# A retention layer and two gated products: the head of the kernel reordered, state scaling moved to ScalarE, a gate clipped from PSUM

## The chip, the cores and the metric

The kernel runs on one core of a Trainium2 chip. The metric is device time of one execution in microseconds. The engines are TensorE (PE, with its weight loads as PEld), VectorE (DVE), ScalarE (ACT), GpSimd (POOL) and SyncE (SP), whose queue issues nearly all transfers.

## The reference

A retention layer over 2 x 8 heads, 768 tokens and head size 64, and then two products with a gate between. Cut to what matters:

```python
# retention, by blocks; lam is one number a head
intra = einsum('bhic,bhjc->bhij', qb, kb) * Dmask      # lam ** (i - j), 0 above the diagonal
out   = einsum('bhij,bhjd->bhid', intra, vb) + einsum('bhid,bhde->bhie', qb * lam_pow, kv_state)
kv_state = lam_block * kv_state + einsum('bhsd,bhse->bhde', kb * rev_pow, vb)
# x: 1536 tokens x 512
h = x @ w_in                                            # 512 x 2048
g = where(h >= 1, h, where(h <= -1, 0, (h + 1)**2 / 4))
y = g @ w_out                                           # 2048 x 512
result = ((y @ w_a) * (y @ w_b)) @ w2_out               # 1536 wide
```

The second half's weights arrive as 8-byte floating point numbers; the kernel makes single precision from them.

## The kernel before, in words

Tokens are taken in 12 chunks of 128. Chunk c has four tiles of 256 KB (`load_chunk`): qT, kT, kn, vn. For each chunk stand, as functions: `att_scores` (TensorE, line 131, two PSUM banks), `att_mask` (kd = kn times a decay, pm = scores times the decay mask, qd = qT times a decay; lines 143, 152, 160), `att_state` (TensorE line 173, then the state is scaled, line 185, and added to, line 188) and `att_out` (TensorE, "inter" from qd and the state at line 199, "intra" from pm and vn at line 203; then the result is split into a high and a low part for the products, ScalarE line 215 and VectorE line 216). Four chunks make up one x tile of 512 tokens (nb = 0, 1, 2).

The decay tables dmask and tabq come from powers of lam: lam is loaded (line 79), powers are taken on GpSimd (line 90), stored to DRAM (`store_powers`, line 99) and read back in a skewed pattern (`tables`, lines 103 and 107).

A weight tile is 512 KB of 8-byte numbers (`load_w`, four buffers named raw). `split_w` makes a pair of tiles of it, a high and a low part: ScalarE hc and c (lines 256, 260), VectorE clip, shift, mask and add (257, 261, 264, 267), ScalarE and GpSimd in `split_act` (288, 289); it ends by issuing the next `load_w`. I call the tiles w0, w1 and so on, in the order in which they are used.

Every product of the two layers is three matmuls (`mm3`, line 277). `h_bank` makes a bank of the first product and its gate: Relu of (h + 1)/2 on ScalarE (296), min with 1 and square on VectorE (297), max with h (298), then `split_act`. `ab_bank`, `y_bank` and `o_bank` are the rest.

The head is written out by hand and ends behind att_out(3). In it the orders of SP and TensorE are as written; a scheduler places the rest, and everything behind the head. `warm(n)` is n matmuls on a tile of zeros. Behind the head the stages run: gate bank by gate bank, with the steps of chunks 4 to 11 and the splits of further weights put between.

Of the kernel before, what the change touches and what calls it, by code (L numbers as in the profile page):

```python
# [8 lines left out]
F32 = mybir.dt.float32  # L9
F32R = mybir.dt.float32r  # L10
BF16 = mybir.dt.bfloat16
I32 = mybir.dt.int32
U32 = mybir.dt.uint32
ACTF = mybir.ActivationFunctionType
ALU = mybir.AluOpType

B, H, S, D = 2, 8, 768, 64
CH = 128
# [16 lines left out]
def retention_ffn_kernel(ctx: ExitStack, tc: tile.TileContext, lam, att, w1i, w1o, w2ab, w2o, out):  # L35
# [6 lines left out]
    nc = tc.nc  # L42
# [3 lines left out]
    win_p = ctx.enter_context(tc.tile_pool(name="win", bufs=8))  # L46
# [10 lines left out]
    def t2(name):  # L57
        return t2_p.tile([128, 512], F32, tag="t2", name=name)
# [5 lines left out]
    exf = const.tile([128, 8], F32, name="exf")  # L64
# [12 lines left out]
    def powers():  # L77

        nc.sync.dma_start(out=lamp, in_=bass.AP(tensor=lam.tensor, offset=lam.offset, ap=[[1, H], [0, 16], [1, 1]]))
        nc.gpsimd.iota(exi, pattern=[[1, 8]], base=0, channel_multiplier=8)  # L80
        nc.vector.memset(base, 0.0)
        nc.vector.memset(zrow[:, 0:CH], 0.0)
        nc.vector.memset(zrow[:, CH:CH + 1], 1.0)
        nc.vector.memset(half, 0.5)
        nc.scalar.dma_start(out=rows[:, 0:CH + 1], in_=zrow)
        nc.vector.tensor_scalar(out=exi, in0=exi, scalar1=127, scalar2=None, op0=ALU.bitwise_and)
        nc.vector.tensor_copy(exf, exi)
        nc.vector.tensor_scalar(out=exf, in0=exf, scalar1=1.0, scalar2=None, op0=ALU.add)
        nc.vector.tensor_scalar(out=base, in0=base, scalar1=lamp, scalar2=None, op0=ALU.add)
        nc.gpsimd.tensor_tensor(out=base, in0=base, in1=exf, op=ALU.pow)  # L90

    def warm(n):

        ps = bank()
        for i in range(n):
            nc.tensor.matmul(out=ps, lhsT=idle[:, 0:128], rhs=idle, start=True, stop=True)
# [23 lines left out]
    def load_chunk(c, parts=(0, 1, 2, 3)):  # L120
        t = ck.setdefault(c, [None] * 4)
        for i in parts:
            t[i] = acc_p.tile([128, 512], F32, tag="acc", name=("qT", "kT", "kn", "vn")[i])
            nc.sync.dma_start(out=t[i], in_=att[c, i])
# [14 lines left out]
    def att_mask(c):  # L139
        cc = c % CPB  # L140
        if cc < CPB - 1:
            kd[c] = t2("kd")
            (nc.vector if c == 0 else nc.gpsimd).tensor_tensor(  # L143
                out=kd[c].rearrange("p (a e d) -> p a e d", a=H // 2, e=2),
                in0=ck[c][2].rearrange("p (a e d) -> p a e d", a=H // 2, e=2),
                in1=dmask[:, :, CH - 1:CH].rearrange("p (a e) i -> p a e i", e=2).to_broadcast([128, H // 2, 2, D]),
                op=ALU.mult,
            )
        pm[c] = []
        for i in range(2):  # L150
            p = t2("pm")
            nc.vector.tensor_tensor(  # L152
                out=p.rearrange("p (a i) -> p a i", a=H // 2), in0=sc[c][i].rearrange("p (a i) -> p a i", a=H // 2),
                in1=dmask.rearrange("p (a e) i -> p e a i", e=2)[:, i], op=ALU.mult,
            )
            pm[c].append(p)
        del sc[c]
        if cc:
            qd[c] = t2("qd")
            (nc.vector if c == 3 else nc.gpsimd).tensor_tensor(  # L160
                out=qd[c], in0=ck[c][0], in1=tabq.rearrange("p a i -> p (a i)"), op=ALU.mult
            )

    def att_state(c):
        cc = c % CPB
        if cc == CPB - 1:
            return
        u = bank()
        k = kd.pop(c)

        for h in range(H):
            p0, pr = 64 * (h % 2), h // 2
            nc.tensor.matmul(  # L173
                out=u[p0:p0 + 64, pr * D:(pr + 1) * D],
                lhsT=k[:, h * D:(h + 1) * D],
                rhs=ck[c][3][:, h * D:(h + 1) * D],
                start=True,
                stop=True,
            )
        u4 = u[:, 0:H // 2 * D].rearrange("p (a e) -> p a e", a=H // 2)  # L180
        old, new = st[cc % 3], st[(cc + 1) % 3]
        if cc == 0:
            nc.vector.tensor_copy(new, u4)
        else:
            nc.gpsimd.tensor_tensor(
                out=new, in0=old, in1=tabq[:, :, CH - 1:CH].to_broadcast([128, H // 2, D]), op=ALU.mult
            )
            nc.vector.tensor_tensor(out=new, in0=new, in1=u4, op=ALU.add)

    def att_out(c):  # L190
# [40 lines left out]
    def load_w():  # L231
        if nxt["load"] >= len(order):
            return
        key = order[nxt["load"]]
        nxt["load"] += 1
        r = raw_p.tile([128, 1024], I32, tag="raw", name="raw")
        nc.sync.dma_start(out=r, in_=srcs[key[0]][key[1]].bitcast(I32))
        raws[key] = r

    def split_w():  # L240
        if nxt["split"] >= len(order):
            return
        key = order[nxt["split"]]
        nxt["split"] += 1
        if key not in raws:
            load_w()
        r = raws.pop(key).rearrange("p (c w) -> p c w", w=2)
        low, high = r[:, :, 0], r[:, :, 1]
        pool, tag = (win_p, "win") if key[0][1] == "i" else (wout_p, "wout")
        w = pool.tile([128, 2, 512], F32R, tag=tag, name=tag)  # L250


        hc = t2_p.tile([128, 512], I32, tag="t2", name="hc")
        v = t2_p.tile([128, 512], I32, tag="t2", name="v")
        c = t2_p.tile([128, 512], I32, tag="t2", name="c")
        nc.scalar.activation(out=hc.bitcast(F32), in_=high.bitcast(F32), func=ACTF.Abs)  # L256
        nc.vector.tensor_scalar(  # L257
            out=hc.bitcast(F32), in0=hc.bitcast(F32), scalar1=HIGH_MIN, scalar2=HIGH_MAX, op0=ALU.max, op1=ALU.min
        )
        nc.scalar.activation(out=c, in_=low.bitcast(U32), func=ACTF.Copy, scale=2.0**-29)  # L260
        nc.vector.tensor_scalar(  # L261
            out=v, in0=hc, scalar1=3, scalar2=0x3FFFFFFF, op0=ALU.logical_shift_left, op1=ALU.bitwise_and
        )
        nc.vector.scalar_tensor_tensor(  # L264
            out=v, in0=high, scalar=-0x40000000, in1=v, op0=ALU.bitwise_and, op1=ALU.bitwise_or
        )
        nc.vector.tensor_tensor(out=v, in0=v, in1=c, op=ALU.add)  # L267
        split_act(v.bitcast(F32), w[:, 0], w[:, 1])
        wt[key] = w
        load_w()  # L270


    def mm3(ps, pairs):
# [5 lines left out]
    def product_in(kind, ft, nb):  # L279

        ps = bank()
        w, x = wt[kind, ft], xy[nb]
        mm3(ps, [([w[:, a, k * 128:(k + 1) * 128] for a in range(2)], [x[:, b, k, :] for b in range(2)])
                 for k in range(KT)])
        return ps

    def split_act(src, hi, lo):
        nc.scalar.copy(hi, src)  # L288
        nc.gpsimd.tensor_tensor(out=lo, in0=src, in1=hi.bitcast(F32), op=ALU.subtract)  # L289
# [2 lines left out]

    def h_bank(ft, nb):
        ps = product_in("1i", ft, nb)
        r = t2("r")
        nc.scalar.activation(out=r, in_=ps, func=ACTF.Relu, scale=0.5, bias=half)  # L296
        nc.vector.scalar_tensor_tensor(out=r, in0=r, scalar=1.0, in1=r, op0=ALU.min, op1=ALU.mult)  # L297
        nc.vector.tensor_tensor(out=r, in0=r, in1=ps, op=ALU.max)
        g = g_p.tile([128, 2, 512], F32R, tag="g", name="g")
        split_act(r, g[:, 0], g[:, 1])  # L300
        gt[1, ft, nb] = g
# [46 lines left out]
                r0 = nb * TB + m * 128  # L348
                nc.sync.dma_start(out=out[r0:r0 + 128, cols], in_=acc_tile[:, cols])

    with tc.manual_schedule(engines={mybir.EngineType.SP, mybir.EngineType.PE}):
        powers()
        nc.vector.memset(idle, 0.0)
        load_chunk(0, (0, 1))
        load_chunk(1, (0, 1))
        load_chunk(2, (0, 1))
        store_powers()
        load_chunk(0, (2, 3))
        tables()
        load_chunk(1, (2, 3))  # L360
        load_chunk(3, (0, 1))
        load_chunk(2, (2, 3))
        load_w()
        load_chunk(3, (2, 3))
        load_w()
        warm(10)
        for c in range(3):
            att_scores(c)
        warm(4)
        att_mask(0)  # L370
        att_state(0)
        att_mask(1)
        att_out(0)
        att_state(1)
        att_scores(3)
        att_mask(2)
        att_out(1)
        att_state(2)
        split_w()
        att_mask(3)  # L380
        att_out(2)
        att_state(3)
        load_chunk(4)
        att_out(3)
        split_w()
        load_chunk(5)


# [114 lines left out]
```

## Time and profile before

| | us |
|---|---|
| median of 3 runs | 631.24 (629.97 to 631.33) |
| profiled execution | 629.82 |
| its span, first to last instruction | 628.0 |
| TensorE busy | 610.6 (97% of the span) |
| VectorE, ScalarE, GpSimd busy | 375.7, 247.6, 246.5 |
| data moved | 52.71 MB, 84 GB/s over the span |

A busy TensorE is one that has a matmul in its pipeline; it says nothing of the clock. The granted clock, as a share of full speed, stands in its own row of the page. Its two levels are 1.2 and 2.4 GHz. The share of busy time is a mean over the whole span, and the head is a seventh of it, so the head is read by stretches and by the chain of work that ended last.

### The profile page before, as it was taken

The numbers are of one execution on the slowest core, as the hardware profiler recorded it, in microseconds if no ns is written. First come the engines' busy times: TensorE is split into PE (matmuls) and PEld (weight loads), VectorE is DVE, ScalarE is ACT, GpSimd is POOL, SyncE is SP. The second block draws the span as 40 slices with busy tenths as digits, with TensorE's granted clock in tenths as the row PEclk, the third lists the DMA queues.
The fourth block names the chain that finished last, engine by engine and source line by source line (L and its number), as shares of the span: only waits on it lengthen the run. The fifth ranks groups of instructions, "written<-read, shape, count | busy, mean of one in ns | idle before, by whom it ended". The sixth has DMA issues, their size and how long they took to land.

```text
span 628.0 us, 8231 instructions
## 1 busy us (share of the span) xinstructions
PE 610.6 (97%) x3171; PEld 501.9 (80%) x3172; DVE 375.7 (60%) x558; ACT 247.6 (39%) x421; POOL 246.5 (39%) x196
## 2 busy tenths in 40 slices
PE   5889899999999999999999999999999999999998
PEld 2768678888888888888888888888888888888886
DVE  0899792585787788679743333555555555555324
ACT  0344344455345435435453455333333333333110
POOL 1756662443352454335675333333322223333210
PEclk9899899999999999999999999999999999999999
DMA  6997210211111122123111221111121111210013
GB/s 192 390 335 261 64 63 24 68 67 68 67 68 55 67 80 68 33 68 101 52 49 34 68 67 68 67 68 67 68 68 67 55 57 58 67 34 1 1 67 135
DMA packets 20503, 52.71 MB, mean 84 GB/s; under 512 B 2408, under 2 KB 4208, under 8 KB 20464
## 3 DMA queue, kind: packets, MB, share of 16 engines
q1 hardware_dynamic: 20448, 52.18, 24.3%
q8 instruction: 25, 0.41, 0.3%
q14 instruction: 14, 0.11, 0.1%
q10 hardware_dynamic: 16, 0.00, 0.0%
HBM read 49.02 MB, written 3.15 MB: 83 GB/s over the span
## 4 chain that ended last, share of the span: by engine, by line
PE 93%; DMA 3%; DVE 2%; POOL 1%; issue 1%; ACT 0%; SPq 0%; DVEq 0%; POOLq 0%
PE ps L277 89%; PE ps L203 2%; PE ps L199 1%; PE ps L131 1%; DMA raw<-in_w1i 1%; DMA tabq<-rows 1%; DMA lamp<-in_lam 1%; PE ps L173 1%; DMA rows<-base 0%; POOL base L90 0%; DVE pm L152 0%; DVE v L261 0%; POOL kd L143 0%; POOL qd L160 0%; DVE x L216 0%
## 5 line engine op out<-in xcount | busy, mean ns | idle before, releaser
L277 PE MATMUL ps<-y,win 128*128 128x512 f32 x864 | 198.8, 389 | 0.0
L277 PEld LDWEIGHTS ps<-y,win 128*128 128x128 f32 x864 | 162.2, 188 | 33.6
L277 PE MATMUL ps<-x,win 128*128 128x512 f32 x576 | 137.1, 396 | 2.3 <-ACT x L215 1.8
L277 PE MATMUL ps<-g,wout 128*128 128x512 f32 x576 | 132.6, 389 | 0.0
L277 PEld LDWEIGHTS ps<-x,win 128*128 128x128 f32 x576 | 109.0, 190 | 26.6 <-ACT x L215 1.9
L277 PEld LDWEIGHTS ps<-g,wout 128*128 128x128 f32 x576 | 108.1, 188 | 22.5 <-issue 0.2
L289 POOL TENSOR_TENSOR win<-v,win 128x512 fp32r<-128x512 f32 x40 | 52.7, 1317 | 151.0 <-ACT win L288 151.0
L277 PE MATMUL ps<-wout,g 128*128 128x512 f32 (+1 forms) x438 | 100.7, 386 | 0.0
L289 POOL TENSOR_TENSOR g<-r,g 128x512 fp32r<-128x512 f32 x48 | 66.5, 1385 | 86.1 <-ACT g L288 60.8
L257 DVE TENSOR_SCALAR hc<-hc 128x512 f32<-128x512 f32 x68 | 36.9, 542 | 102.2 <-ACT hc L256 102.2
L277 PEld LDWEIGHTS ps<-wout,g 128*128 128x128 f32 x438 | 81.6, 188 | 16.7
L321 DVE TENSOR_TENSOR acc<-acc,ps 128x512 f32<-128x512 f32 (+1 forms) x97 | 64.8, 679 | 47.6 <-PE ps L277 47.5
L289 POOL TENSOR_TENSOR wout<-v,wout 128x512 fp32r<-128x512 f32 x28 | 36.7, 1312 | 85.2 <-ACT wout L288 85.0
L264 DVE SCALAR_TENSOR_TENSOR v<-raw,v 128x512 int32<-128x512 int32 x68 | 68.0, 1000 | 2.2
L297 DVE SCALAR_TENSOR_TENSOR r<-r 128x512 f32<-128x512 f32 x48 | 37.7, 786 | 50.3 <-ACT r L296 50.2
L267 DVE CUSTOM_DVE_ANT_0 v<-v,c 128x1024 uint16<-128x1024 uint16 x68 | 55.6, 818 | 6.3
L306 ACT COPY a<-ps 128x512 f32<-128x512 f32 x36 | 21.1, 587 | 95.3 <-PE ps L277 94.0
L288 ACT CAST win<-v 128x512 fp32r<-128x512 f32 x40 | 24.9, 621 | 84.7 <-DVE v L267 84.7
L289 POOL TENSOR_TENSOR g<-a,g 128x512 fp32r<-128x512 f32 x36 | 46.5, 1291 | 25.8 <-ACT g L288 25.8
L296 ACT ACTIVATE r<-ps,half 128x512 f32<-128x512 f32 x48 | 32.8, 684 | 47.2 <-PE ps L277 47.2
L261 DVE TENSOR_SCALAR v<-hc 128x512 int32<-128x512 int32 x68 | 44.5, 654 | 4.3
L256 ACT ACTIVATE hc<-raw 128x512 f32<-128x512 f32 x68 | 45.3, 665 | 2.0 <-DMA raw<-in_w1i 2.0
(45 smaller groups left out, 375.2 us busy)
## 6 DMA issues: line engine op xcount, KB each, us to landing
raw<-in_w2ab SPq DMA_DIRECT2D x24, 512.0 KB, 3.2
raw<-in_w1i SPq DMA_DIRECT2D x16, 512.0 KB, 3.3
raw<-in_w1o SPq DMA_DIRECT2D x16, 512.0 KB, 3.3
raw<-in_w2o SPq DMA_DIRECT2D x12, 512.0 KB, 3.4
qT<-in_att SPq DMA_DIRECT2D x12, 256.0 KB, 4.8
kT<-in_att SPq DMA_DIRECT2D x12, 256.0 KB, 5.0
kn<-in_att SPq DMA_DIRECT2D x12, 256.0 KB, 5.5
vn<-in_att SPq DMA_DIRECT2D x12, 256.0 KB, 5.7
```

The lines of the kernel that those rows point to most:

```text
L256: nc.scalar.activation(out=hc.bitcast(F32), in_=high.bitcast(F32), func=ACTF.Abs)
L257: nc.vector.tensor_scalar(out=hc.bitcast(F32), in0=hc.bitcast(F32), scalar1=HIGH_MIN, scalar2=HIGH_MAX, op0=ALU.max, op1=ALU.min)
L261: nc.vector.tensor_scalar(out=v, in0=hc, scalar1=3, scalar2=0x3FFFFFFF, op0=ALU.logical_shift_left, op1=ALU.bitwise_and)
L264: nc.vector.scalar_tensor_tensor(out=v, in0=high, scalar=-0x40000000, in1=v, op0=ALU.bitwise_and, op1=ALU.bitwise_or)
L267: nc.vector.tensor_tensor(out=v, in0=v, in1=c, op=ALU.add)
L277: nc.tensor.matmul(out=ps, lhsT=l[a], rhs=r[b], start=(i == 0 and j == 0), stop=(i == n - 1 and j == 2))
L288: nc.scalar.copy(hi, src)
L289: nc.gpsimd.tensor_tensor(out=lo, in0=src, in1=hi.bitcast(F32), op=ALU.subtract)
L296: nc.scalar.activation(out=r, in_=ps, func=ACTF.Relu, scale=0.5, bias=half)
L297: nc.vector.scalar_tensor_tensor(out=r, in0=r, scalar=1.0, in1=r, op0=ALU.min, op1=ALU.mult)
L306: nc.scalar.copy(a, pa)
L321: nc.vector.tensor_tensor(out=total, in0=total, in1=ps, op=ALU.add)
```

## The change

Seven edits:

- `powers`: lam is no longer added to a zeroed tile on VectorE; the power reads it directly. The zeroing of the tile for `warm` comes first.
- The order of loads in the head: chunk 0's qT and kT, then w0 and w1, chunk 0's kn and vn, chunk 1's qT and kT, then the store of the powers and the tables. Chunk 2 is loaded whole behind chunk 1's kn and vn, w2 behind it, then chunk 3 and w3.
- `split_w` is cut in three, `split_begin`, `split_middle` (which now issues the next load) and `split_end`. w0 and w1 are split ahead of att_mask(0), w2 and w3 between the last steps of the head.
- att_scores(2) stands behind att_state(0), att_scores(3) behind att_out(1); 20 idle matmuls instead of 4 stand behind att_scores(1).
- The state scaling goes from one GpSimd operation to four on ScalarE, 64 elements each. qd of chunk 3 goes from VectorE to GpSimd.
- The gate: VectorE clips h from PSUM to -1 and 1, ScalarE takes ((c + 1)/2) squared, VectorE the max with h.
- In the head all engines now follow the written order, not SP and TensorE alone.

```diff
-        nc.vector.tensor_scalar(out=base, in0=base, scalar1=lamp, scalar2=None, op0=ALU.add)
-        nc.gpsimd.tensor_tensor(out=base, in0=base, in1=exf, op=ALU.pow)
+        nc.gpsimd.tensor_tensor(out=base, in0=lamp.to_broadcast([128, 8]), in1=exf, op=ALU.pow)
...
-            (nc.vector if c == 3 else nc.gpsimd).tensor_tensor(
+            nc.gpsimd.tensor_tensor(
                 out=qd[c], in0=ck[c][0], in1=tabq.rearrange("p a i -> p (a i)"), op=ALU.mult
...
-            nc.gpsimd.tensor_tensor(
-                out=new, in0=old, in1=tabq[:, :, CH - 1:CH].to_broadcast([128, H // 2, D]), op=ALU.mult
-            )
+            for pr in range(H // 2):
+                nc.scalar.mul(new[:, pr], old[:, pr], tabq[:, pr, CH - 1:CH])
             nc.vector.tensor_tensor(out=new, in0=new, in1=u4, op=ALU.add)
...
+    def split_begin(key):
...
         nc.scalar.activation(out=hc.bitcast(F32), in_=high.bitcast(F32), func=ACTF.Abs)
+        nc.scalar.activation(out=c, in_=low.bitcast(U32), func=ACTF.Copy, scale=2.0**-29)
+        half_split[key] = high, hc, c
+
+    def split_middle(key):
...
         nc.vector.tensor_tensor(out=v, in0=v, in1=c, op=ALU.add)
-        split_act(v.bitcast(F32), w[:, 0], w[:, 1])
+        half_split[key] = v
+        load_w()
+
+    def split_end(key):
...
+        split_act(half_split.pop(key).bitcast(F32), w[:, 0], w[:, 1])
         wt[key] = w
-        load_w()
...
         r = t2("r")
-        nc.scalar.activation(out=r, in_=ps, func=ACTF.Relu, scale=0.5, bias=half)
-        nc.vector.scalar_tensor_tensor(out=r, in0=r, scalar=1.0, in1=r, op0=ALU.min, op1=ALU.mult)
+        nc.vector.tensor_scalar(out=r, in0=ps, scalar1=-1.0, scalar2=1.0, op0=ALU.max, op1=ALU.min)
+        nc.scalar.activation(out=r, in_=r, func=ACTF.Square, scale=0.5, bias=half)
         nc.vector.tensor_tensor(out=r, in0=r, in1=ps, op=ALU.max)
...
-    with tc.manual_schedule(engines={mybir.EngineType.SP, mybir.EngineType.PE}):
+    with tc.manual_schedule():
         powers()
-        nc.vector.memset(idle, 0.0)
         load_chunk(0, (0, 1))
+        load_w()
+        load_w()
+        load_chunk(0, (2, 3))
         load_chunk(1, (0, 1))
-        load_chunk(2, (0, 1))
         store_powers()
-        load_chunk(0, (2, 3))
         tables()
         load_chunk(1, (2, 3))
-        load_chunk(3, (0, 1))
-        load_chunk(2, (2, 3))
+        load_chunk(2)
         load_w()
-        load_chunk(3, (2, 3))
+        load_chunk(3)
         load_w()
+        w0, w1, w2, w3 = order[:4]
+        nxt["split"] = 4
         warm(10)
-        for c in range(3):
-            att_scores(c)
-        warm(4)
+        att_scores(0)
+        att_scores(1)
+        warm(20)
+        split_begin(w0)
+        split_begin(w1)
+        split_middle(w0)
+        split_end(w0)
+        split_middle(w1)
+        split_end(w1)
         att_mask(0)
         att_state(0)
+        att_scores(2)
         att_mask(1)
         att_out(0)
         att_state(1)
-        att_scores(3)
         att_mask(2)
         att_out(1)
+        att_scores(3)
         att_state(2)
-        split_w()
+        split_begin(w2)
         att_mask(3)
         att_out(2)
         att_state(3)
+        split_middle(w2)
         load_chunk(4)
+        split_begin(w3)
         att_out(3)
-        split_w()
+        split_end(w2)
+        split_middle(w3)
+        split_end(w3)
         load_chunk(5)
```

SP's queue in the second half of the head, before: from w0's load (raw_145) to w3's (raw_385). raw is a weight tile; 147 and 149 are the rest of chunk 3, and 346 to 352 are chunk 4.

```order
L237 DMA raw_145<-in_w1i 128x1024
L124 DMA kn_147<-in_att 128x512
L124 DMA vn_149<-in_att 128x512
L237 DMA raw_151<-in_w1i 128x1024
L237 DMA raw_306<-in_w1i 128x1024
L124 DMA qT_346<-in_att 128x512
L124 DMA kT_348<-in_att 128x512
L124 DMA kn_350<-in_att 128x512
L124 DMA vn_352<-in_att 128x512
L237 DMA raw_385<-in_w1i 128x1024
```

And of the change, from w2's load (raw_143, the third) through chunk 3 and w3 to chunk 4 (398 and 400):

```order
L235 DMA raw_143<-in_w1i 128x1024
L123 DMA qT_145<-in_att 128x512
L123 DMA kT_147<-in_att 128x512
L123 DMA kn_149<-in_att 128x512
L123 DMA vn_151<-in_att 128x512
L235 DMA raw_153<-in_w1i 128x1024
L235 DMA raw_220<-in_w1o 128x1024
L235 DMA raw_230<-in_w1o 128x1024
L235 DMA raw_396<-in_w1o 128x1024
L123 DMA qT_398<-in_att 128x512
L123 DMA kT_400<-in_att 128x512
```

Before, three weight tiles were loaded ahead of chunk 4; now seven are, the last three w4, w5 and w6 (220, 230, 396).

TensorE in the head, before, the first state group (173) and the four groups behind it:

```order
L173 MATMUL ps<-vn,kd 64x64 x8
L203 MATMUL ps<-pm,vn 64x128 x8
L173 MATMUL ps<-vn,kd 64x64 x8
L131 MATMUL ps<-qT,kT 128x128 x8
L199 MATMUL ps<-qd,st_94 64x128 x8
```

And of the change (172 state, 130 scores, 201 intra, 197 inter):

```order
L172 MATMUL ps<-vn,kd 64x64 x8
L130 MATMUL ps<-qT,kT 128x128 x8
L201 MATMUL ps<-pm,vn 64x128 x8
L172 MATMUL ps<-vn,kd 64x64 x8
L197 MATMUL ps<-qd,st_94 64x128 x8
```

The scores of chunk 2 moved from ahead of the tables to between state(0) and out(0); those of chunk 3 from here to behind out(1).

## Rows read from the trace of the kernel before

**Rows 1.** The chain that ended last: start us, us, what.

```profile
5.49 1.66 POOL base L90
7.16 2.50 DMA rows<-base
...
10.66 5.58 DMA tabq<-rows
...
91.56 533.43 PE ps L277 x2358
```

**Rows 2.** Stretches: us, busy us (instructions) by engine, PEclk, DMA share, GB/s.

```profile
8.00:10.00 2.00, 1.85 (x32) 1.68 (x30) 0.00 (x0) 0.00 (x0) 0.00 (x0) 1.00 0.79 80
...
16.00:20.00 4.00, 3.74 (x50) 3.67 (x52) 2.97 (x6) 0.58 (x1) 2.55 (x3) 0.57 1.06 389
...
50.00:60.00 10.00, 10.00 (x106) 8.00 (x106) 9.76 (x14) 5.80 (x10) 7.35 (x7) 0.99 0.93 333
```

**Rows 3.** TensorE in order of time, 5 to 33 us: start us, us, what.

```profile
6.41 1.16 PE L131 MATMUL ps<-qT,kT 64*128 64x128 f32 x16 [0.60 <-DMA kT<-in_att]
...
9.08 1.16 PE L131 MATMUL ps<-qT,kT 64*128 64x128 f32 x16 [0.15 <-DMA kT<-in_att]
...
17.14 2.03 PE L203 MATMUL ps<-pm,vn 128*64 128x128 f32 x15
...
30.71 2.08 PE L131 MATMUL ps<-qT,kT 64*128 64x128 f32 x16
32.72 3.32 PE L277 MATMUL ps<-x,win 128*128 128x512 f32 x12
```

**Rows 4.** The chain that ended last, 44 to 71 us.

```profile
44.61 1.42 POOL qd L160
...
46.07 1.40 PE ps L199 x16
...
49.37 3.34 PE ps L277 x12
52.71 1.09 PE ps L131 x16
53.80 0.61 PE ps L173 x16
...
55.29 2.95 PE ps L277 x12
...
60.97 1.02 PE ps L203 x16
...
66.48 4.38 PE ps L277 x11
```

**Rows 5.** Waits, 0 to 92 us, TensorE and SP's queue: us, times, longest.

```profile
PE ps L277 <- ACT x L215: 1.8, 1, 1.8
...
SPq L237 <- DVE v L264: 40.6, 8, 13.9
```

**Rows 6.** VectorE in order of time, 36 to 42 us.

```profile
36.98 0.42 DVE L257 TENSOR_SCALAR hc<-hc 128x512 f32<-128x512 f32 x1
...
38.37 0.69 DVE L264 SCALAR_TENSOR_TENSOR v<-raw,v 128x512 int32<-128x512 int32 x1
...
41.88 0.41 DVE L188 TENSOR_TENSOR st<-st,ps 128x256 f32<-128x256 f32 x1
```

**Rows 7.** Groups by line: busy us, mean ns of one, idle before.

```profile
L297 DVE SCALAR_TENSOR_TENSOR r<-r 128x512 f32<-128x512 f32 x48 | 37.7, 786 | 50.3 <-ACT r L296 50.2
...
L298 DVE TENSOR_TENSOR r<-r,ps 128x512 f32<-128x512 f32 x48 | 32.6, 678 | 0.2
...
L160 POOL TENSOR_TENSOR qd<-qT,tabq 128x512 f32<-128x512 f32 x9 | 12.7, 1408 | 0.0
...
L215 ACT CAST x<-ps 128x512 fp32r<-128x512 f32 x12 | 7.0, 580 | 20.7 <-PE ps L203 20.7
```

**Rows 8.** DMA issues of the whole span: KB each, median us to landing.

```profile
raw<-in_w1i SPq DMA_DIRECT2D x16, 512.0 KB, 3.3
```

More of the change, by code (lines that the diff above doesn't have):

```diff
@@ L80, in powers @@
         nc.gpsimd.iota(exi, pattern=[[1, 8]], base=0, channel_multiplier=8)
-        nc.vector.memset(base, 0.0)
+        nc.vector.memset(idle, 0.0)
         nc.vector.memset(zrow[:, 0:CH], 0.0)
@@ L238, in load_w @@
         raws[key] = r
[L240 to L244, printed above, removed]
+    half_split = {}
+    def split_begin(key):
         if key not in raws:
@@ L248, in split_w @@
         low, high = r[:, :, 0], r[:, :, 1]
-        pool, tag = (win_p, "win") if key[0][1] == "i" else (wout_p, "wout")
-        w = pool.tile([128, 2, 512], F32R, tag=tag, name=tag)
         hc = t2_p.tile([128, 512], I32, tag="t2", name="hc")
-        v = t2_p.tile([128, 512], I32, tag="t2", name="v")
         c = t2_p.tile([128, 512], I32, tag="t2", name="c")
         nc.scalar.activation(out=hc.bitcast(F32), in_=high.bitcast(F32), func=ACTF.Abs)
+        nc.scalar.activation(out=c, in_=low.bitcast(U32), func=ACTF.Copy, scale=2.0**-29)
+        half_split[key] = high, hc, c
+    def split_middle(key):
+        high, hc, c = half_split[key]
+        v = t2_p.tile([128, 512], I32, tag="t2", name="v")
         nc.vector.tensor_scalar(
@@ L259, in split_w @@
         )
-        nc.scalar.activation(out=c, in_=low.bitcast(U32), func=ACTF.Copy, scale=2.0**-29)
         nc.vector.tensor_scalar(
@@ L267, in split_w @@
         nc.vector.tensor_tensor(out=v, in0=v, in1=c, op=ALU.add)
-        split_act(v.bitcast(F32), w[:, 0], w[:, 1])
-        wt[key] = w
-        load_w()
+        half_split[key] = v
+        load_w()
+    def split_end(key):
+        pool, tag = (win_p, "win") if key[0][1] == "i" else (wout_p, "wout")
+        w = pool.tile([128, 2, 512], F32R, tag=tag, name=tag)
+        split_act(half_split.pop(key).bitcast(F32), w[:, 0], w[:, 1])
+        wt[key] = w
+    def split_w():
+        if nxt["split"] >= len(order):
+            return
+        key = order[nxt["split"]]
+        nxt["split"] += 1
+        split_begin(key)
+        split_middle(key)
+        split_end(key)
     def mm3(ps, pairs):
```

## The prediction

> **What bounds the kernel now.** I read the chain that ended last first. From 91.56 us to the end it is TensorE alone: 2358 matmuls in 533.43 us, 0.226 us each [rows 1]. Nothing before 91.56 us reaches past it except by delaying it, and none of the edits makes those matmuls shorter. So the change is decided in the head, the first 91.56 us. The profiled execution took 629.82 us with a span of 628.0; it stands 1.42 below the median of 631.24, so I make the sum in microseconds gained or lost and put it on the median. About 0.2% (1.3 us) is what a measurement of this kernel can tell from no change.
>
> Then I split the head at the first gate matmul (line 277), which starts at 32.72 [rows 3]. What stands behind it up to 91.56 is a fixed list: 8 gate banks, 7 score groups, 6 state groups, 7 inter and 8 intra groups. At full clock they take 2.95, 1.09, 0.61 and, inter as intra, 1.02 us [rows 4], so 23.6 + 7.6 + 3.7 + 7.1 + 8.2 = 50.2 us. It took 91.56 - 32.72 = 58.84. The other 8.6 us are two stalls, each with a stretch at half clock behind it. The second is chunk 7's: 1.8 us of waiting for ScalarE's copy [rows 5], then 4.38 for 11 matmuls, where 11 of 12 parts of 2.95 are 2.70: 3.5 together. The first takes the other 5.1: TensorE waits until GpSimd's qd, 44.61 to 46.03, and the groups behind it take 1.40 and 3.34 instead of 1.02 and 2.95 [rows 4]. Behind these stalls is VectorE, busy for 9.76 of 10 us from 50 to 60 [rows 2].
>
> Up to 32.72 the chain is: the powers (1.66), their store (2.50), tables (5.58) [rows 1], then chunk by chunk. TensorE's third score group ran at 9.08, long before the tables; out(0) started at 17.14 [rows 3].
>
> **The change, part by part, up to the first gate bank.**
>
> *Powers.* exi and exf no longer queue behind the wait for lam and one VectorE operation goes, so the power can start before 5.49 [rows 1]. That is worth nothing: the store of the powers now has eight loads ahead on SP's queue after the first pair, among them two weight tiles of 512 KB. Three score groups started from 6.41 to 9.08, each behind its pair of 256 KB tiles, so a pair lands every 1.33 us [rows 3]. Weights counted as a pair each, the eight loads are four pairs: 6.4 + 5.3 = 11.7. The store lands at about 11.9 instead of 9.66 [rows 1]. Part of the delay is paid by the gap that it fills: from 8 to 10 us the queue moved 80 GB/s [rows 2].
>
> *Tables.* From the end of the store to the end of the tables' piece it took 16.24 - 9.66 = 6.6 us [rows 1], with one pair of loads (1.3) ahead that is now already in. The tables are in at 17.2 to 18.5; I take 18.1.
>
> *Splits of w0 and w1.* They run from about 8 to 16 us on ScalarE, VectorE and GpSimd, which were empty there: none of them did anything from 8 to 10 us [rows 2], and their next work waited for the tables. Cost nothing; if the tables came before 14 us they would delay kd(0) by the rest of a split, up to 3 us.
>
> *16 more idle matmuls.* At 0.22 to 0.43 us each they end by 19.5. The next thing that TensorE needs is chunk 2's kT (below, 20.8), so they cost nothing; without that cover up to 2 us.
>
> *Scores of chunk 2.* They now stand between state(0) and out(0), and chunk 2's qT and kT come behind the tables and chunk 1's kn and vn: 18.1 + 2 x 1.33 = 20.8. So out(0) starts at 21.9, not 17.14, and TensorE then works without a gap: out(0) 0.9, state(1) 0.6, out(1) 2.0, scores(3) 1.1, state(2) 0.6, out(2) 2.0. out(2) ends at 29.2.
>
> *Chunk 4's load.* This is the term that decides. SP works in order. Each middle part of a split now issues the next weight load, so w4, w5 and w6 stand ahead of chunk 4 on SP. There are four raw buffers: w6 takes w2's, so SP waits at w6 until VectorE's mask operation of w2's split has read it. SP has lost 40.6 us in 8 waits of just this kind already [rows 5], but chunk 4 was ahead of them. Behind out(2): ScalarE's copy 0.58 [rows 7], the four state scalings that are now on ScalarE, VectorE's state add 0.41, clip 0.42, shift at most the same, mask 0.69 [rows 6]. For one scaling of 64 elements before has no row. Above it is a copy of 512, 0.58; below I allow nothing. VectorE's 256 and 512 elements (0.41 and 0.68 [rows 6, 7]) would put a fixed part at 0.14, so I take 0.25, four of them 1.0. The mask ends at 29.2 + 0.6 + 1.0 + 1.5 + 0.4 for hand-overs = 32.7. A weight load lands 3.3 us after its issue [rows 8]: 36.1; behind it qT and kT, 1.33: 37.5. Scores(4) stood at 30.71 and waited for no transfer [rows 3]. They took 2.08 there, twice their 1.09, at half clock behind an idle TensorE; after a wait of some five microseconds I price them so again. The first gate bank starts at 39.7: **7.0 later**.
>
> The price of a small ScalarE operation is also stated: the Trainium skill, "ScalarE: Activation LUTs", section "What ACT_TABLE_LOAD costs", gives 280 ns plus 0.833 ns an element with a pointer operand and an overlap of 93 ns, an estimate of 1.05 us for four, by which the sum would stay within 0.1; no run here shows it yet.
>
> *qd(3) on GpSimd.* It costs GpSimd 1.41 [rows 7] and is early enough, as out(3) comes late. Worth nothing behind the later wait.
>
> **After the first gate bank.** With w0 to w3 split by 38 us, VectorE does not carry w2 and w3 (34 to 41 us) beside chunks 4 and 5. The first stall stood behind them: g's subtraction, then qd at 44.61 [rows 4]. It goes with the half clock behind it: -5.0. The second stays and grows: chunk 7's copy on ScalarE now queues behind four scalings that wait for VectorE's add (+1.0), and GpSimd's qd of chunks 6 and 7 come later in its queue (one qd, +1.4 [rows 7]). Waits 8.6 - 5.0 + 2.4 = 6.0 instead of 8.6: **2.5 back**, with bounds from the rows of 0 and 8.6.
>
> *The gate.* Relu on ScalarE, min and square on VectorE (0.786) and max (0.678) become clip, Square, max. The clip reads PSUM, as max does, so I take 0.68 on VectorE; an SBUF clip without a wait takes 0.42 [rows 6, 7]. Behind 91.56 us TensorE is never late and a bank's chain only gains a hand-over: nothing. In the head it saves VectorE 8 x 0.1 = 0.8 us, already inside the 2.5.
>
> Here a rule speaks against the edit: the Trainium skill, "VectorE: DVE Perf Modes", section "Why PSUM operands drop a tier", says that fp32 from PSUM runs at the single rate. By it the clip is 0.68 and the saving 0.8; by the SBUF row it would be 0.42 and 8 x 0.36 = 2.9, and the sum up to 2 us better. The PSUM rows agree with the rule.
>
> **Sum.** +7.0 - 2.5 = +4.5: 634.3 for an execution like the profiled one, 635.7 on the median.
>
> **Rivals.**
> 1. *VectorE's backlog was the whole of it (faster).* After the first gate bank TensorE then never waits: 39.7 + 50.2 = 89.9, 1.7 us earlier than 91.56: 629.6. For it: 9.76 of 10 us [rows 2], and that the two splits moved ahead are the same length as the two that stood before the first stall. Against: chunk 7's stall hangs on its own state and copy, which get an extra queue. It decides when the waits after the first gate bank fall under 1.5 us.
> 2. *The two cancel (no change).* Chunk 4's kT lands at 33 (w6's buffer free 4.5 us earlier, since out(2) and the scalings are quicker than I sum): +2.5 - 2.5 = 631.2. Against: out(2) cannot end before chunk 2 has come, which is behind the tables.
> 3. *The half clock spreads (slower still).* TensorE waits from 33 to 37 and runs the scores and the first bank at 1.2 GHz, and chunk 7's stall keeps another; if also the stretch after the idle matmuls falls to it (the granted clock was 0.57 from 16 to 20 us, at 1.2 GHz for most of it, after TensorE had been idle [rows 2]), out(2) ends 1.7 later and everything behind: with the first stall only half gone, +4.5 + 1.7 + 2.5 = 640.
>
> **How the numbers follow.** My forecast 0.66, rival 1 0.11, rival 2 0.09, rival 3 0.14. Slower 0.80, same 0.09, faster 0.11. The low end is scalings at nothing (-1.0), scores at full clock (-1.0) and no growth of the second stall (-2.4): 631.3, taken to 631.0; the high end is rival 3, 640.0. Under the low end are rival 1 and a part of rival 2, above the high end a few in a hundred.
>
> **What would show it.** In the changed profile: the score group of chunk 2 waits for kT near 21; SP waits some 3 us for VectorE's mask before w6; scores(4) start near 37.5, released by a transfer of kT; the first gate bank near 39.7; no stall at 43; one of some 3 us before chunk 7's gate bank; dense from about 96. I am wrong if scores(4) start before 34, or if the dense stretch has gaps.

## The result, and the profile after

The changed kernel takes **637.38 us** (median of 4 runs, 637.1 to 638.31) where the kernel before took 630.9 beside it: ratio 1.0112, 95% interval 1.0096 to 1.0128. That is 6.5 us slower. The forecast was 635.7, and the result lies inside its range of 631.0 to 640.0. The profiled execution took 637.62 with a span of 635.7. One number further down needs a word: of the four executions of the version "both mends" one was disturbed (1246.2 us); its median counts it, its ratio doesn't.

The chain that ended last, of the changed kernel (start us, us, what):

```profile
6.63 5.11 DMA rows<-base
...
20.83 1.16 PE ps L130 x16
...
28.25 1.07 PE ps L201 x16
29.35 0.58 ACT x L213
29.93 0.97 ACT st L185 x4
...
33.09 0.18 SPq L235
...
33.79 4.29 DMA kT<-in_att
...
38.22 2.08 PE ps L130 x16
40.30 4.45 PE ps L289 x12
...
71.63 1.06 ACT st L185 x4
72.69 0.48 ACT x L213
...
73.94 4.40 PE ps L289 x11
...
99.24 533.43 PE ps L289 x2358
```

Against [rows 1] the last piece is the same to the hundredth, 2358 matmuls in 533.43 us: behind the head nothing changed, the new gate included. It starts at 99.24 instead of 91.56. (That is 7.7 later, more than the 6.5 between the medians; the profiled execution of before was 1.1 below its median.)

TensorE in order of time, with its waits, against [rows 3]:

```profile
38.22 2.08 PE L130 MATMUL ps<-qT,kT 64*128 64x128 f32 x16 [6.43 <-DMA kT<-in_att]
40.23 4.52 PE L289 MATMUL ps<-x,win 128*128 128x512 f32 x12
...
66.47 1.09 PE L197 MATMUL ps<-qd,st 64*64 64x128 f32 x16 [1.71 <-POOL qd L159]
...
73.21 0.50 PE L289 MATMUL ps<-x,win 128*128 128x512 f32 x1 [2.92 <-ACT x L213]
73.94 4.38 PE L289 MATMUL ps<-x,win 128*128 128x512 f32 x11 [0.22 <-DVE x L214]
...
88.53 0.69 PE L172 MATMUL ps<-vn,kd 128*64 128x64 f32 x16 [0.37 <-POOL kd L142]
```

The first gate bank starts at 40.23, 7.5 later than 32.72. From there to the dense stretch (the 2358 matmuls that run to the end without a gap) it takes 59.0 us, where it took 58.84. So the whole loss lies ahead of the first gate bank, and nothing of it comes back behind. SyncE's queue shows the place: three issues of weight loads (w4, w5, w6) that take 11.82 us, and chunk 4 behind them (SP in order of time).

```profile
21.45 11.82 SPq L235 DMA_DIRECT2D raw<-in_w1o  x3
33.36 0.38 SPq L123 DMA_DIRECT2D qT<-in_att  x1
33.79 0.42 SPq L123 DMA_DIRECT2D kT<-in_att  x1
```

The three issues end at 33.27 and one takes 0.33, so w6's own starts at 32.94: SP had stood before it for 10.4 us. The mask of w2's split, which reads the buffer that w6 needs, ends 0.07 earlier, at 32.87 (VectorE in order of time):

```profile
32.18 0.69 DVE L262 SCALAR_TENSOR_TENSOR v<-raw,v 128x512 int32<-128x512 int32 x1
```

(The chain above comes to SP's 33.09 by an operation of ScalarE for w3 that ended just then. As w6's issue had begun before, that can't be what released it.)

Stretches, as in [rows 2] (us; busy us of PE, PEld, DVE, ACT, POOL; PEclk, DMA share, GB/s):

```profile
8.00:10.00 2.00, 0.00 (x0) 0.00 (x0) 1.44 (x3) 1.92 (x4) 0.00 (x0) 0.84 1.04 404
...
30.00:40.00 10.00, 3.57 (x46) 3.18 (x42) 6.92 (x11) 4.69 (x13) 3.15 (x3) 0.83 0.59 199
40.00:50.00 10.00, 10.00 (x87) 7.82 (x84) 5.68 (x9) 2.99 (x5) 4.02 (x4) 0.83 1.03 366
50.00:60.00 10.00, 10.00 (x115) 8.01 (x113) 9.04 (x12) 3.55 (x6) 5.38 (x5) 1.00 0.66 227
60.00:70.00 10.00, 8.29 (x106) 6.76 (x106) 8.98 (x14) 5.51 (x12) 5.45 (x5) 1.00 0.76 254
```

The gap of the queue from 8 to 10 us is filled as the prediction said (404 GB/s for 80), with splits on VectorE and ScalarE in it. But the time that this frees on VectorE later on is not used: VectorE idles with TensorE from 30 to 50, and from 50 to 70 it is full again, 9.04 and 8.98 of 10, as in the kernel before.

### The profile page after: what moved, and what is told of

Read it like the earlier page. It is cut to its first block, busy times and chain, and to the rows that moved or that the text cites. A ratio compares the mean times of both kernels' runs of the same rounds, so it can differ in the third digit from the quotient of the medians.

```text
span 635.7 us, 8307 instructions
## 1 busy us (share of the span) xinstructions
PE 614.0 (97%) x3188; PEld 502.5 (79%) x3188; DVE 363.4 (57%) x555; ACT 258.2 (41%) x453; POOL 237.1 (37%) x189
## 4 chain that ended last, share of the span: by engine, by line
PE 91%; DMA 4%; ACT 1%; issue 1%; SPq 1%; DVE 1%; POOL 1%; POOLq 0%; DVEq 0%
PE ps L289 87%; DMA kT<-in_att 1%; PE ps L201 1%; PE ps L130 1%; PE ps L197 1%; DMA rows<-base 1%; DMA qT<-in_att 1%; DMA lamp<-in_lam 1%; SPq L123 1%; PE ps L172 0%; ACT st L185 0%; POOL base L89 0%; ACT x L213 0%; DVE x L214 0%; POOL g L301 0%
## 5 line engine op out<-in xcount | busy, mean ns | idle before, releaser
L301 POOL TENSOR_TENSOR g<-r,g 128x512 fp32r<-128x512 f32 x48 | 63.1, 1316 | 124.7 <-ACT g L300 120.7
L256 DVE TENSOR_SCALAR hc<-hc 128x512 f32<-128x512 f32 x68 | 41.9, 617 | 109.4 <-ACT hc L247 108.5
L265 DVE CUSTOM_DVE_ANT_0 v<-v,c 128x1024 uint16<-128x1024 uint16 x68 | 58.4, 858 | 4.8
L309 DVE TENSOR_SCALAR r<-ps 128x512 f32<-128x512 f32 x48 | 32.8, 683 | 49.5 <-PE ps L289 49.5
L310 ACT ACTIVATE r<-r,half 128x512 f32<-128x512 f32 x48 | 34.7, 723 | 63.3 <-DVE r L309 63.3
L262 DVE SCALAR_TENSOR_TENSOR v<-raw,v 128x512 int32<-128x512 int32 x68 | 53.0, 779 | 1.8
L300 ACT CAST g<-r 128x512 fp32r<-128x512 f32 x48 | 29.8, 621 | 45.6 <-DVE r L311 45.5
```

The source lines that it names most:

```text
L256: nc.vector.tensor_scalar(out=hc.bitcast(F32), in0=hc.bitcast(F32), scalar1=HIGH_MIN, scalar2=HIGH_MAX, op0=ALU.max, op1=ALU.min)
L262: nc.vector.scalar_tensor_tensor(out=v, in0=high, scalar=-0x40000000, in1=v, op0=ALU.bitwise_and, op1=ALU.bitwise_or)
L309: nc.vector.tensor_scalar(out=r, in0=ps, scalar1=-1.0, scalar2=1.0, op0=ALU.max, op1=ALU.min)
L310: nc.scalar.activation(out=r, in_=r, func=ACTF.Square, scale=0.5, bias=half)
```

## Experiments: the queue

**w4 to w7 behind chunks 4 and 5.** Of the changed kernel one thing undone: the middle parts of the splits in the head issue no load.

```diff
-    def split_middle(key):
+    def split_middle(key, load=True):
...
-        load_w()
+        if load:
+            load_w()
...
-        split_middle(w0)
+        split_middle(w0, load=False)
...
         load_chunk(5)
+        for _ in range(4):
+            load_w()
```

> The changed kernel with one thing undone: w4 to w7 are issued behind chunks 4 and 5 instead of ahead of them; everything else stays. Theory of the prediction (the queue is the loss, +7.0 before the first gate bank): scores(4) no longer wait for a transfer of kT and start near 31 to 32, the first gate bank near 33 instead of 40.23, at full clock; with nothing coming back later the dense stretch starts 6 to 7 earlier than 99.24, so about 631 us. Rival A (what follows out(2) on VectorE and ScalarE sets the pace whatever the queue does): the first gate bank comes at 33 but the waits before chunk 7 grow by as much, and the time stays at 636 to 638. Rival B (the late tables and scores(2) are the loss): the first gate bank stays behind 36.

Measured: 630.81 us, ratio to before 0.9998 (0.9985 to 1.0011). TensorE in order of time:

```profile
31.37 1.16 PE L130 MATMUL ps<-qT,kT 64*128 64x128 f32 x16
33.28 0.49 PE L290 MATMUL ps<-x,win 128*128 128x512 f32 x1 [0.76 <-ACT x L213]
...
59.62 1.16 PE L197 MATMUL ps<-qd,st 64*64 64x128 f32 x16 [2.50 <-POOL qd L159]
...
66.36 0.49 PE L290 MATMUL ps<-x,win 128*128 128x512 f32 x1 [1.36 <-ACT x L213]
67.09 4.38 PE L290 MATMUL ps<-x,win 128*128 128x512 f32 x11 [0.23 <-DVE x L214]
```

Scores(4) wait for nothing, run in 1.16 instead of 2.08, and the first gate bank stands at 33.28. The dense stretch starts at 92.28, again 59.0 behind it. Undoing the order of the queue takes the whole loss away. Rivals A and B fall: the late tables and scores(2) cost 0.6 us together (33.28 against 32.72), and the waits behind the first gate bank neither shrink nor grow.

**The same three tiles behind chunk 4, ahead of chunk 5.** 

```diff
-        split_middle(w2)
+        split_middle(w2, load=False)
         load_chunk(4)
+        load_w()
+        load_w()
+        load_w()
```

w0's and w1's middle parts issue none either; w3's still does.

> The changed kernel with w4, w5 and w6 behind chunk 4 but still ahead of chunk 5. If the wait of chunk 4 alone is the price: first gate bank near 33, dense near 93, about 631 us, as in the kernel with both chunks ahead. If any chunk behind the three tiles pays the same: first gate bank near 33, then a wait of some 6 us for chunk 5's kT at the next score group, and the time stays within 1 us of 637.4.

Measured: 636.84 us, ratio 1.0094 (1.0081 to 1.0107).

```profile
33.77 0.49 PE L290 MATMUL ps<-x,win 128*128 128x512 f32 x1 [0.74 <-ACT x L213]
34.50 2.79 PE L290 MATMUL ps<-x,win 128*128 128x512 f32 x11 [0.23 <-DVE x L214]
44.56 2.08 PE L130 MATMUL ps<-qT,kT 64*128 64x128 f32 x16 [7.26 <-DMA kT<-in_att]
...
73.50 2.83 PE L290 MATMUL ps<-x,win 128*128 128x512 f32 x11 [0.22 <-DVE x L214]
```

The gate bank is early and the wait moves on by one chunk: 7.26 us for chunk 5's kT. So the price does not belong to chunk 4: the chunk that stands next behind the weight loads that wait pays it, here chunk 5.

**Only w6 and w7 behind; w4 and w5 stay ahead of chunk 4.** 

```diff
-        split_middle(w2)
+        split_middle(w2, load=False)
...
-        split_middle(w3)
+        split_middle(w3, load=False)
...
         load_chunk(5)
+        load_w()
+        load_w()
```

> The changed kernel with w4 and w5 still ahead of chunk 4 and only w6 and w7 behind chunk 5. The prediction put the loss down to w6, the one load that has to wait for VectorE's mask of w2's split. If that wait is it: scores(4) start near 31.4, first gate bank near 33.3, about 631 us, as in the kernel with all of w4 to w7 behind. If the bytes ahead of chunk 4 are it (two tiles of 512 KB, 1.33 us each): kT of chunk 4 comes 2.7 us later than there and the time is 633 to 634.

Measured: 631.08 us, ratio 1.0001 (0.999 to 1.0013). In the trace scores(4) start at 32.03 after a wait of 0.46 for kT, the first gate bank at 33.42. So it is not the 1 MB of w4 and w5 ahead of chunk 4 that costs; it is w6 alone, which has to wait for VectorE's mask of w2's split (w7 stood behind chunk 4 already). That step of the prediction is shown.

## Experiments: what should have come back

**The changed kernel with splits later.** Two of the three splits beside chunks 4 to 7 move behind chunk 7.

```diff
-            plan = {0: base + 7, 1: base + 10, 2: base + 12}
+            plan = {0: base + 7, 1: base + 10, 2: base + 12} if g else {0: 5, 1: 8, 2: 12}
```

> The changed kernel as it is, with the pace of the splits behind the head altered: 5 tiles instead of 7 split by the end of the first four gate banks (so the splits of w5 and w6 move behind chunk 7), 8 instead of 10 by the end of the next four. If the 2.5 us that should have come back are lost to VectorE (its three splits beside chunks 4 to 7 set when chunk 7's copy and GpSimd's qd come): the waits of 1.71 and 2.92 us go and the half clock behind them, dense near 93.5 instead of 99.24, about 631 to 632 us. If the scalings on ScalarE and the late chunk loads set them: 636 to 637.5.

Measured: 630.81 us, ratio 1.0009 (0.9999 to 1.0018). TensorE in order of time, chunk 7's gate bank and the start of the dense stretch:

```profile
40.40 5.07 PE L289 MATMUL ps<-x,win 128*128 128x512 f32 x12
...
69.18 3.00 PE L289 MATMUL ps<-x,win 128*128 128x512 f32 x12
...
93.00 7.21 PE L289 MATMUL ps<-g,wout 128*128 128x512 f32 x29
```

The first gate bank is as late as in the changed kernel (40.40), and still waits for chunk 4. But the waits of 1.71 and 2.92 are gone, no half clock follows, and 52.6 us suffice for the 59.0. Its VectorE is busy for 8.10 and 6.65 of 10 us from 50 to 70 (9.04 and 8.98 in the changed kernel). So the second stall comes from the splits of w5 and w6, which the change leaves where they were; the late chunks, as late here, are not it. A split takes time on ScalarE and GpSimd too, so this run alone does not name the engine. The waits of the changed kernel do (0 to 100 us; us, times, longest): ScalarE stands still until VectorE has done its part of w4 to w6, the second-product weights (wout).

```profile
ACT wout L300 <- DVE v L265: 10.1, 3, 4.1
```

So it is VectorE's backlog that holds chunk 7 up, and not ScalarE's queue.

**The kernel before with splits later.** The same line, `plan`, in the kernel before.

> The kernel before with the altered pace of splits alone. If the backlog on VectorE costs the kernel before as much as the changed one: chunk 7's stall (1.8 us and 1.7 of half clock) goes, the first stall at 44 stays, as it stands behind the splits of w2 and w3: 627 to 629 us. Against it: two more splits stand behind chunk 7 and may come late for the second product, with small gaps in the dense stretch.

Measured: 628.08 us, ratio 0.9962 (0.9949 to 0.9975), as expected. Chunk 7's stall is gone: its gate bank takes 3.02 without a wait. The first stall stays (2.26 us for GpSimd's qd), a wait of 2.83 for qd(3) stays, and the dense stretch has one gap of 0.63, for a high-low pair of a second-product weight. 2.6 us are gained, not 6.6.

**Both mends on the changed kernel.** The edits of the first and of the fourth experiment together.

> Both edits together on the changed kernel: w4 to w7 behind chunks 4 and 5, and the splits of w5 and w6 behind chunk 7. If queue and VectorE's backlog are two separate prices, they add: first gate bank at 33.3, then 50 to 53 us without a stall over 1 us, dense near 85, 623 to 625 us, faster than both kernels. If the one only hides the other: 629 to 631.

Measured: **624.07 us**, ratio 0.9895 (0.9878 to 0.9911), 6.6 us faster than before.

```profile
33.69 0.51 PE L290 MATMUL ps<-x,win 128*128 128x512 f32 x1 [0.76 <-ACT x L213]
...
60.84 3.07 PE L290 MATMUL ps<-x,win 128*128 128x512 f32 x12
...
84.75 11.54 PE L290 MATMUL ps<-g,wout 128*128 128x512 f32 x48
```

51.1 us from the first gate bank to the dense stretch, against the 50.2 of work that the prediction counted. The two prices are separate: 637.38 less 6.6 for the queue, less 6.6 for the backlog is 624.2.

## Experiments: the other parts

**State scaling back on GpSimd.** 

```diff
-            for pr in range(H // 2):
-                nc.scalar.mul(new[:, pr], old[:, pr], tabq[:, pr, CH - 1:CH])
+            nc.gpsimd.tensor_tensor(
+                out=new, in0=old, in1=tabq[:, :, CH - 1:CH].to_broadcast([128, H // 2, D]), op=ALU.mult
+            )
```

> The changed kernel with the state scaling back on GpSimd as one operation. Theory of the prediction: ScalarE's four scalings stand ahead of w2's split (1.0 us before w6 is issued) and ahead of chunk 7's copy (1.06 us): 1 to 2 us less, 635.5 to 636.5. Rival: GpSimd's operation (0.8 us) queues behind kd and qd and is as late: no change, 637.4 within 0.5.

Measured: 636.84 us, ratio 1.0098 (1.0085 to 1.0111), not to be told from the changed kernel's 1.0112 (1.0096 to 1.0128). Its profile has nearly the same stalls (6.70, 1.67 and 2.54, where the changed kernel has 6.43, 1.71 and 2.92). That the scalings cost 1 to 2 us is not borne out.

**The old gate.** 

```diff
-        nc.vector.tensor_scalar(out=r, in0=ps, scalar1=-1.0, scalar2=1.0, op0=ALU.max, op1=ALU.min)
-        nc.scalar.activation(out=r, in_=r, func=ACTF.Square, scale=0.5, bias=half)
+        nc.scalar.activation(out=r, in_=ps, func=ACTF.Relu, scale=0.5, bias=half)
+        nc.vector.scalar_tensor_tensor(out=r, in0=r, scalar=1.0, in1=r, op0=ALU.min, op1=ALU.mult)
```

> The changed kernel with the old gate (Relu from PSUM on ScalarE, min and square on VectorE, max). Theory of the prediction: a gate bank takes 0.1 us more of VectorE, eight in the head, so up to 0.8 slower, 637.4 to 638.2. Rival: the new gate's Square waits on ScalarE for VectorE's clip and holds chunk 7's copy behind it, so that the old gate is 1 to 2 us faster, 635.5 to 636.5. From the dense stretch on no change by either.

Measured: 639.62 us, ratio 1.0141 (1.0128 to 1.0154): the new gate is worth some 2.2 us by the medians, more than my 0.8, and the rival has the wrong sign. (The two intervals touch at 1.0128, so the size is not exact.) The groups by line (busy us, mean ns of one), of the changed kernel,

```profile
L309 DVE TENSOR_SCALAR r<-ps 128x512 f32<-128x512 f32 x48 | 32.8, 683 | 49.5 <-PE ps L289 49.5
```

and of this one:

```profile
L310 DVE SCALAR_TENSOR_TENSOR r<-r 128x512 f32<-128x512 f32 x48 | 37.6, 783 | 59.2 <-ACT r L309 59.1
```

give the 0.1 us a bank that the prediction had (0.683 for 0.783). The rest stands in chunk 7's stall, TensorE in order of time:

```profile
74.66 5.79 PE L289 MATMUL ps<-x,win 128*128 128x512 f32 x12 [4.67 <-ACT x L213]
```

4.67 us for 2.92, and 5.79 for its 12 matmuls, which took 0.50 and 4.38 in the changed kernel. Ahead of it the old min-and-square takes 1.28 us in one bank, beside GpSimd's work, and 0.69 in the next, with GpSimd idle: VectorE, in order of time.

```profile
63.20 1.28 DVE L310 SCALAR_TENSOR_TENSOR r<-r 128x512 f32<-128x512 f32 x1 [1.27 <-ACT r L309]
...
70.64 0.69 DVE L310 SCALAR_TENSOR_TENSOR r<-r 128x512 f32<-128x512 f32 x1
```

**The old gate with both mends.** The edits of "both mends" and of "the old gate".

> The changed kernel with both mends (w4 to w7 behind chunks 4 and 5, two splits later) and the old gate. If the gate is worth something only while VectorE is behind: within 1 us of 624.07. If it is worth its 2.2 us there too: 626.3.

Measured: 624.8 us, ratio 0.9905 (0.9892 to 0.9919), within 1 us of the new gate's 624.07 and not to be told from it. In the changed head the gate is worth some 2.2 us while VectorE is behind, and nothing that can be shown once it isn't.

**New gate and ScalarE's scaling in the head before.** The two diffs on the scaling and the gate, read the other way, on the kernel before.

> The kernel before with the new gate and the scaling on ScalarE, its head as it was. The old gate cost the changed kernel 2.2 us, through VectorE's backlog ahead of chunk 7, and GpSimd's scaling gave it 0.6 back. If these are worth the same wherever VectorE is behind: about -2.2 + 0.6, so 629 us. If the four scalings ahead of chunk 7's copy weigh as much as the gate saves: 630 to 631, no change.

Measured: 631.95 us, ratio 1.0017 (1.0008 to 1.0026): no gain, and rather a loss of 1 us. Chunk 7's stall is 4.11 us here, 1.8 in [rows 5], and the first expectation is wrong: prices taken from one order did not carry over to the other. ScalarE's four scalings (1.06) stand ahead of chunk 7's copy; how much of the 4.11 is theirs was not tried apart.

**These two and the later splits in the head before.** The same with the line `plan` as well.

> The kernel before, its head as it was, with the new gate, the scaling on ScalarE and the splits of w5 and w6 behind chunk 7. It tells what the new order of the head is worth once its queue is mended: the same three in the changed head gave 624.07. If two splits ahead of the tables are worth their length on VectorE where it is behind (the first stall at 44): 626 to 627 here. If they are worth nothing once the backlog is thinned: 624 here too.

Measured: 624.81 us, ratio 0.9906 (0.9893 to 0.992), not to be told from the 624.07 with the changed head. No gain of the new order of the head is shown, even mended (0.7 us between the medians, intervals that overlap); gate, scaling and pace give the gain. By the traces the two heads differ, but their differences nearly cancel: the old one reaches its first gate bank at 31.64, 2.0 us earlier than "both mends" (33.69), and takes 54.0 us from there to the dense stretch (85.68) instead of 51.1. Why gate and scaling give 3.3 us here (628.08 without them) and none without the later splits, these runs don't settle.

**The store of the powers earlier,** with both mends.

```diff
         load_w()
-        load_w()
         load_chunk(0, (2, 3))
+        store_powers()
         load_chunk(1, (0, 1))
-        store_powers()
+        load_w()
         tables()
```

> The changed kernel with both mends, and the store of the powers moved up in SP's queue: w1 and chunk 1's qT and kT, three quarters of a tile pair each way, now stand between the store and the tables instead of ahead of the store. The store landed at 11.74 with eight loads ahead of it; with five ahead (1.33 us for 512 KB) it lands 2 to 2.7 earlier, near 9.5, and the tables with it, since SP waits 4.4 us for the store now and loads in that time instead. If the tables set the head: 2 us less than 624.07, about 622. If chunk 2's loads set it, which stay as many: 624.

Measured: 623.82 us, ratio 0.9887 (0.9872 to 0.9902), no difference. SP issued the first table at 9.89 instead of 11.78. Most of that was lost on the way: the two halves of dmask took 5.0 and 6.0 us from issue to landing, where they took 3.5 and 4.2 with both mends alone. They were in by 16.3 at the latest, against 16.4. And the two engines that wait for the tables stood elsewhere, TensorE and VectorE in order of time:

```profile
12.57 2.08 PE L130 MATMUL ps<-qT,kT 64*128 64x128 f32 x16 [4.81 <-DMA kT<-in_att]
14.58 6.06 PE L95 MATMUL ps<-idle 128*128 128x512 bf16 x19
20.57 0.69 PE L172 MATMUL ps<-vn,kd 128*64 128x64 f32 x16
21.18 1.16 PE L130 MATMUL ps<-qT,kT 64*128 64x128 f32 x16
```

```profile
16.25 1.53 DVE L265 CUSTOM_DVE_ANT_0 v<-v,c 128x1024 uint16<-128x1024 uint16 x1
17.70 0.68 DVE L142 TENSOR_TENSOR kd<-kn,dmask 128x512 f32<-128x512 f32 x1
```

The idle matmuls, which the prediction priced at nothing because chunk 2's kT came behind them, are now what state(0) and scores(2) follow without a gap. And kd(0) starts at 17.70 behind the end of w1's split, not earlier than the 16.53 with both mends alone: the delay that the prediction named for tables that come early. Both covers are used up, so the run does not show what earlier tables would be worth without them.

## Why the prediction was right, and where it wasn't

*The loss ahead of the first gate bank (+7.0; +7.5 measured).* Step by step: store landed at 11.7 (11.9 forecast), scores(2) at 20.83 (20.8), out(2) over at 29.3 (29.2), four scalings 0.97 (1.0), chunk 4's kT in at 38.1 (37.5), scores(4) in 2.08 as priced. The runs without w6's wait show the mechanism. One detail was off. I wrote that SP would wait "some 3 us" for w6; it waited 10.4, since SP came to w4 at 21.45 and not near 30. That made no difference, because the mask's end decides.

*What comes back (2.5; 0 measured).* This term was mis-sized. (8.6 - 6.0 is 2.6; the sum carried 2.5.) The waits behind the first gate bank are 59.0 - 50.2 = 8.8, where "waits 8.6 - 5.0 + 2.4 = 6.0" had been forecast: 1.5 of half clock in the first gate bank, 1.71 for qd, 2.92 + 0.22 for chunk 7's x, 1.55 of half clock behind it (4.38 against the 2.83 of the second experiment for the same 11 matmuls), 0.37 for kd, and some 0.5 in small pieces.

Against the kernel before, piece by piece: The first stall is gone, as forecast; there is none at 43 to 46. But it was worth 3.8 us and not 5.0, a wait of 2.24 and 1.6 of half clock in the three groups behind it (TensorE of the kernel before in order of time):

```profile
46.07 1.40 PE L199 MATMUL ps<-qd,st 64*64 64x128 f32 x16 [2.24 <-POOL qd L160]
```

The prediction had taken for it whatever chunk 7's stall left of the 8.6, small pieces from elsewhere included. Chunk 7's stall grew from 3.8 (1.78 + 0.49 of waits, 1.55 of half clock) to 6.4, by 2.6 where 2.4 had been forecast. And the first gate bank ran at half clock for much of its 4.52 us, where it took 3.32 before: 1.2 that had been put at nothing. -3.8 + 2.6 + 1.2 leaves nothing.

That the growth has the forecast size is luck, for its cause was another. I had put it down to the scalings and to GpSimd's qd queueing behind one more qd. Without the scalings on ScalarE it was nearly the same; with two splits fewer it was gone, the wait for qd with it. The backlog of w4 to w6 on VectorE, which this term left out, held those waits in place. The first experiment says the same: there chunk 4 is in time and the first gate bank runs at full clock, and still nothing comes back, because chunk 7's waits (2.50, 1.36 and 0.23) and the half clock behind them grow by as much as the first stall gave.

Why VectorE is so full there the traces suggest too. The shift of a split took 0.43 us at 31.72, with GpSimd idle, and 1.37 at 65.33, beside a qd on GpSimd that ran from 64.97 for 1.44 (VectorE of the changed kernel in order of time):

```profile
31.72 0.43 DVE L259 TENSOR_SCALAR v<-hc 128x512 int32<-128x512 int32 x1
...
65.33 1.37 DVE L259 TENSOR_SCALAR v<-hc 128x512 int32<-128x512 int32 x1
```

The Trainium skill, "SBUF — State Buffer", section "Who interferes with whom", says that such an operation can need a pair of ports that VectorE shares with GpSimd, and that the one that issues first has it for its whole instruction; these two rows agree. No run here takes GpSimd's work away to show it.

*The gate.* Its price was right (0.683 us, as the PSUM rows had it), its worth was not: some 2.2 us instead of 0.8, most of it in chunk 7's stall. The 0.683 agrees with the rule that the prediction took from the Trainium skill, "VectorE: DVE Perf Modes", section "Why PSUM operands drop a tier".

*The scalings.* 1.06 us for four in the rows, where mine was 1.0. The estimate from the Trainium skill, "ScalarE: Activation LUTs", section "What ACT_TABLE_LOAD costs", was 1.05. But moving them off ScalarE could not give back 1.0 ahead of w6: VectorE's state add waited only 0.27 for them, since VectorE's own subtraction for out(2) (0.69 from 29.97), which the sum left out, runs beside them (VectorE in order of time).

```profile
30.93 0.42 DVE L186 TENSOR_TENSOR st<-st,ps 128x256 f32<-128x256 f32 x1 [0.27 <-ACT st L185]
```

*The rivals.* Rival 1 (no wait behind the first gate bank) is what the changed kernel becomes with its splits later, and 630.81 is near its 629.6; as it stands it has 8.8 us of waits. Rival 2 needed chunk 4's kT at 33; it came at 38.1. Of rival 3 half came true: half clock in scores(4), in the first gate bank and at chunk 7, but none from 16 to 20 us, where the granted clock was 0.98.

## What to carry to other kernels

On a queue that works in order, look at which issue can wait, and for whom: here one weight load that needed its buffer back made TensorE wait 6.4 us for the input of the next stage, while the bytes ahead of that input cost next to nothing. Work that is moved earlier on an engine pays only if that engine's next burst gets thinner; here VectorE idled where it had been relieved and was as full as ever where it was late. And a step that costs nothing because something hides it (idle matmuls, an early split) has its price back as soon as the cover is improved away.

## What was not expected of the hardware

The same wait was followed by different clocks. In the changed kernel chunk 7's gate bank came after 2.92 us of waiting and its last 11 matmuls took 4.38 us; in the second experiment it came after 2.92 as well, and they took 2.83. What differs in the rows before is that the changed kernel had also waited 1.71 us, until 66.47, and the other had not. That is no rule, though: the kernel before had no such wait in the 15 us ahead of chunk 7's stall, waited 1.78 + 0.49 us there, and its 11 matmuls took 4.38 as well [rows 4]. Why the clock fell in two of these and not in the third stays open. Likewise in the second experiment TensorE, after 7.26 us of idling, ran two groups at half clock (scores, 2.08, then state, 1.12) and was back at full clock in the next one, while the changed kernel stayed at half clock through most of a gate bank after 6.43 us. A wait of 0.46 us (only w6 behind) left the clock alone: scores(4) took 1.16.
